# Four of the sixteen filter products of layer 2 on GpSimd, evictions moved from ScalarE to VectorE, and a new order of the items between the layers

## Chip, cores and metric

The kernel runs on one core of a Trainium2 chip. The metric is the device time of one execution in microseconds (us); the time of the kernel before is the median of three runs. The profile is of one further execution.

## What is computed

A sequence of 2048 rows of 448 bf16 values goes through two layers. Each layer has a spectral half (a two-dimensional Fourier transform of the normalized rows, a product with complex filter weights, the transform back, the residual) and a feed-forward half (448 to 1792, squared ReLU, back to 448, the residual). Both layers use the same weights.

```python
def _A_ref(x, w_r, w_i):
    X = rfft2(x)
    X = X * (w_r + 1j * w_i)
    return irfft2(X, s=(S, D))

def _B_ref(x, w1, b1, w2, b2):
    h = einsum("bsd,df->bsf", x, w1) + b1
    r = where(h > 0, h, 0)
    return einsum("bsf,fd->bsd", r * r, w2) + b2

x = x + _A_ref(layernorm(x), w_r, w_i)
x = x + _B_ref(layernorm(x), w1, b1, w2, b2)
x = x + _A_ref(layernorm(x), w_r, w_i)
x = x + _B_ref(layernorm(x), w1, b1, w2, b2)
```

## The kernel before

Everything stays in on-chip memory between the layers. The Fourier transforms are matmuls with constant matrices, split into stages, and each stage ends in PSUM and is copied ("evicted") to SBUF as bf16 by ScalarE (ACTIVATE, line 764) or VectorE (CAST, line 765). A layer runs through these stages:

- A: the transform of each tile of 128 rows along the sequence (`first_A` in layer 1, `second_A`, lines 1228 to 1245, in layer 2), 16 tiles, evicted into `XA`. In layer 2 tile 15 is evicted in two halves, and each half serves half of the columns.
- TD (`stage_TD`, line 934): the transform along the 448 columns, over 16 blocks n, alone or two at a time. It needs `XA` of all sixteen tiles. Evicted into `U`, a part of `arena`.
- B (`stage_B`, line 959): the rest of the sequence transform, two blocks at a time, evicted into `EF`, another part of `arena`.
- W (`stage_W`, line 988): the product with the filter, one instruction for each block n. It multiplies the 448 values of a block, read twice through a broadcast view, by 896 values of the weights `Wt`, both in SBUF, and writes 896 bf16 values into `T3`, a part of `wide`. In the kernel before all sixteen run on VectorE (line 793).
- Bi (`stage_Bi`, line 993): the first step back, for pairs of blocks v = 0 to 7. Bi v needs the two products n = 2v and 2v+1. Evicted into `VT`.
- TI, AI (lines 1019 and 1041): the rest of the way back; TI needs all of `VT`, that is, all eight Bi. Then the normalization (`ln_B`), the two feed-forward matmuls (`h_part`, `h_pairs`, `o_tile`) and the residual. The last tiles of this half (`o_tile`, then folding and statistics on VectorE) feed the next layer's A.

The text of the program only adds work units with their reads and writes; `_Sched` (line 297) puts them into queues. Each unit has a number, counted as the program adds it. The order on every engine is written out by hand in `ORDER` (line 140) as lists of these numbers, one list for each of TensorE ("pe"), ScalarE ("act"), VectorE ("dve"), GpSimd ("pool") and the DMA queue of SyncE ("sp"). An engine runs its list strictly in that order, and waits at a unit whose inputs are not there. A unit with an `alt` may stand in the list of any engine that its `alt` names; where the planner's own reckoning sees a gap on TensorE, it puts filler matmuls there (`warm_mm`, line 1375). The costs in the program are used for that reckoning, for the choice of PSUM banks and for the places of the waits; with the lists written out they do not choose the order.

The numbers of layer 2's spectral half, for following the prediction. Each TD, B and Bi unit is matmuls, and the number behind the slash is that of its eviction:

| stage | units (block: matmuls/eviction) |
|---|---|
| A, tile 15 | two halves: 815/816 and 817 |
| TD | 0: 818/819, 1: 820/821, 2-3: 822/823, 4-5: 833/834, 6-7: 835/836, 8-9: 845/846, 10-11: 847/848, 12-13: 857/858, 14-15: 859/860 |
| B | 0-1: 824/825, 826; 2-3: 829/830; 4-5: 837/838; 6-7: 841/842; 8-9: 849/850; 10-11: 853/854; 12-13: 861/862; 14-15: 865/866, 867 |
| W | n = 0 to 15: 827, 828, 831, 832, 839, 840, 843, 844, 851, 852, 855, 856, 863, 864, 868, 869 |
| Bi | v = 0: 870/871, 872; 1: 873/874; 2: 875/876; 3: 877/878; 4: 879/880; 5: 881/882; 6: 883/884, 885; 7: 886/887, 888 |

Evictions of two blocks have 896 elements a partition, of one block 448; those of a Bi have 1024, or 512 where it is evicted in two halves. In layer 2 before the change, the engines take these units in this order:

- ScalarE: 817 | 834, 860, 823, 850, 838, 836, 854, 825, 866, 858, 830, 880, 842, 882, 887, 862, 876, 872, 871, 878, 884
- VectorE: 816 | 846, 848, 821, 819, 852, 851, 867, 826, 869, 855, 868, 856, 839, 828, 840, 831, 827, 888, 843, 832, 844, 863, 864, 874, 885
- TensorE: 815 | 833, 845, 859, 847, 822, 849, 820, 818, 837, 853, 835, 865, 824, 879, 857, 829, 841, 881, 886, 875, 861, 870, 873, 877, 883

GpSimd's list holds nineteen units, all in layer 1: scalings of a constant matrix for `first_A` (line 776), memsets (line 806) and the four indirect DMAs that load the weights (line 842).

Of the kernel before, what the change touches and what calls it, by code (L numbers as in the profile page):

```python
# [6 lines left out]
ALU = mybir.AluOpType  # L7
# [11 lines left out]
LW = 224  # L19
# [14 lines left out]
def make_constants():  # L34
# [116 lines left out]
1261 1266 1233 1227 1271 1274 1277 1280 1283""",  # L151
    "act": """
# [11 lines left out]
1173 1165 1163 1170 1044 1237 1244 1242 1247 1239 1254 1252 1259 1269 1262 1249 1267 1264 1257""",  # L164
    "dve": """
# [22 lines left out]
1234 1278 1281 1284""",  # L188
    "pool": """
16 48 32 23 40 19 56 95 64 85 20 108 111 22 134 137 21 17 18""",  # L190
    "sp": """
8 9 10 11 12 13 14 15 24 25 26 201 202 141 142 143 144 146 222 223 224 145 225 226 227 272 276 277 294 312 330 348
366 384 934 939 940 957 975 1132 993 1135 1138 1011 1141 1029 1226 1232 1182 1047 1185 1188 1179 1229 1276 1273 1235
# [85 lines left out]
def _res(a):  # L279
    return a.ap() if isinstance(a, _PsAP) else a  # L280
# [350 lines left out]
def _free(ap):  # L631
    n = 1
    for step, cnt in list(ap.ap)[1:]:
        n *= cnt
    return n


def bass_interleave_layers__spectral_gfnet__dense_activation_squared_relu__prompt_kernel(nc, A_x, A_w_r, A_w_i, B_x, B_w1, B_b1, B_w2, B_b2, out):
# [5 lines left out]
    sch = _Sched()  # L644

    with ExitStack() as es:
# [16 lines left out]
        T3 = wide[:, 0:16 * TW].rearrange("p (n w) -> p n w", n=16)  # L663
# [127 lines left out]
        def tt(o, a, b, op, eng="dve"):  # L791
            rate = 0.96 if isinstance(a, _PsAP) or eng == "pool" else 1.92
            sch.add(eng, lambda e: e.tensor_tensor(o, _res(a), b, op), [a, b], [o], cost=_free(o) / rate + 69.0)  # L793
# [18 lines left out]
        def W_at(n):  # L812

            a = WS * 2 + (LW + 1) * (15 - n)
            o = Wt[:, (LW + 1) * n + 1:]
            return bass.AP(o.tensor, o.offset, [list(o.ap[0]), [a - (LW + 1) * n, 2], [WS, 2], [1, LW]])
# [117 lines left out]
        def stage_TD(n0, n, first):  # L934

            t = _Tile(n)
            u = sch.new_unit("pe")
            for i in range(n):
                for g in range(2):
                    for k in range(2):  # L940
                        x = XA[0:P if first else QD, k, g, 4 * (n0 + i):4 * (n0 + i) + 4].rearrange("p c t j -> p (c t j)")
                        if first:
                            r, m = 1 - g, TD_sb[:, g, k, :].rearrange("p (q i) -> p q i", q=2)
                            o = t[lambda b, i=i, r=r: ps[:, b + i, :].rearrange("p (q w) -> p q w", q=2)[:, :, r * QD:(r + 1) * QD]]
                        else:
                            r = (1 - k) if g == 0 else k
                            l0, m = g * 256 + r * QD, TQ_sb[:, g, r, :]
                            o = t[lambda b, i=i, l0=l0: ps[:, b + i, l0:l0 + QD]]
                        mm(o, x, m, g == 0 and k == 0, g == 1 and k == 1, skip=True, unit=u)
            TD_out(t, n0, n, EV["TD"])  # L950
# [34 lines left out]
                for i in range(2):  # L985
                    evac(EF[:, m0 + i, :], t[i][lambda b: ps[:, b, 0:2 * LW]], EV["B"])

        def stage_W(n):

            x = EF[:, n, :].rearrange("p (f l) -> p f l", f=2)[:, :, None, :].to_broadcast([P, 2, 2, LW])  # L990
            tt(T3[:, n, 0:4 * LW].rearrange("p (f w l) -> p f w l", f=2, w=2), x, W_at(n), ALU.mult)

        def stage_Bi(v):

# [257 lines left out]
        def spectral(first):  # L1252
            L = 0 if first else 1

            def rank(k, n):
                sch.bias, sch.tag = PR[k][L] - PR["step"][L] * n, f"{k}{L}.{n}"

            for g in range(4):
                n = 4 * g
                while n < 4 * g + 4:  # L1260
                    w = 2 if n in PAIRS else 1
                    rank("TD", n / 2)
                    stage_TD(n, w, first)
                    n += w
                for m0 in (4 * g, 4 * g + 2):
                    rank("B", m0 / 2)
                    stage_B(m0)
                    for m in (m0, m0 + 1):
                        rank("W", m / 2)
                        stage_W(m)  # L1270
            if first:
                sch.bias, sch.tag = 0.0, ""
                for i in range(2):
                    dma("sp", H_sb[:, 8 * i:8 * i + 8], dc["H"][:, 8 * i:8 * i + 8], after=[U[:, HGATE, 0:1]])
            for v in range(8):
                rank("Bi", v)
                stage_Bi(v)
# [190 lines left out]
```

## Time and profile before

| | |
|---|---|
| median of three runs | 253.97 us (253.86 to 254.29) |
| the profiled execution, its own time | 254.23 us |
| its span, first to last instruction | 252.4 us |
| layer 2, first TD matmul to last Bi matmul | 137.48 to 153.05 us of the span |
| first TI matmul of layer 2 | 153.94 us of the span |

All times inside the kernel are us from the start of the span. The profiled execution took 1.8 us longer than its span, and 0.26 us more than the median. A timeline row gives start, length, engine, source line, operation, output and input, and how many instructions it merges; neighbouring instructions of one engine overlap in the records a little, so the distance from start to start is shorter than the length of one. A group row ends in the busy time, the mean length of one in ns, the idle time before them and what ended it.

### The profile page before, as it was taken

What the parts mean: (1) busy time and instruction counts of PE and PEld (TensorE: products, weight loads), DVE (VectorE), ACT (ScalarE), POOL (GpSimd) and SP (SyncE); (2) the same over time, 40 slices, a digit from 0 to 9 for tenths busy, and PEclk for the clock granted to TensorE, in tenths of its full rate; (3) what the DMA queues carried; (4) which work ended last, traced back from release to release, by engine and by line L of the source; (5) the groups of instructions that cost most, each with busy time, mean ns of one, the idle gap of its engine ahead of it and who ended that gap; (6) DMA issues with size and microseconds to landing.
All of it is one profiled execution on the core that took longest, in us unless ns stands there. A gap on an engine that the chain in (4) does not pass through costs nothing.

```text
span 252.4 us, 6120 instructions
## 1 busy us (share of the span) xinstructions
PE 245.3 (97%) x2454; PEld 157.3 (62%) x2454; DVE 192.9 (76%) x624; ACT 164.2 (65%) x360; POOL 11.0 (4%) x23
## 2 busy tenths in 40 slices
PE   7999999999999999999998999999999999999996
PEld 2688688976446755544567688797544565544454
DVE  3988989999756789999997997999990398122632
ACT  6977979981468873209648998999638884017500
POOL 0880000000000000000000000000000000000000
PEclk9999999999999999999999999999999999999999
DMA  6988379515110001020000000031236010210002
GB/s 193 383 296 289 126 240 245 150 43 75 43 42 3 0 3 43 0 43 3 0 3 1 3 5 0 3 81 43 43 94 65 0 43 23 75 57 0 3 19 91
DMA packets 24080, 18.10 MB, mean 72 GB/s; under 512 B 16082, under 2 KB 22706, under 8 KB 24052
## 3 DMA queue, kind: packets, MB, share of 16 engines
q1 hardware_dynamic: 22756, 13.22, 20.7%
q0 software_dynamic: 576, 3.69, 4.0%
q10 hardware_dynamic: 720, 0.80, 1.0%
q8 instruction: 19, 0.31, 0.5%
q14 instruction: 9, 0.07, 0.1%
HBM read 12.20 MB, written 1.84 MB: 56 GB/s over the span
## 4 chain that ended last, share of the span: by engine, by line
PE 76%; DVE 12%; ACT 7%; DMA 3%; issue 1%
PE ps L739 76%; DVE wide L793 3%; DVE arena L765 3%; ACT XA L764 2%; DMA H_sb<-c_H 2%; DMA xin<-in_A_x_dram 1%; ACT arena L758 1%; ACT wide L764 1%; DVE x_sb L1224 1%; ACT Fs L775 1%; DVE st L864 1%; DVE VT L765 1%; ACT mv L758 1%; ACT wide L887 1%; ACT wide L886 1%
## 5 line engine op out<-in xcount | busy, mean ns | idle before, releaser
L739 PE MATMUL ps<-wide,W_sb 64*128 64x512 bf16 (+1 forms) x770 | 90.8, 346 | 0.0
L739 PE MATMUL ps<-W_sb,arena 128*128 128x448 bf16 (+3 forms) x476 | 87.0, 342 | 0.0
L758 ACT ACTIVATE arena<-ps,b1col 128x512 bf16<-128x512 f32 x84 | 52.8, 687 | 34.2 <-PE ps L739 33.9
L739 PEld LDWEIGHTS ps<-wide,W_sb 64*128 64x128 bf16 (+1 forms) x770 | 54.4, 95 | 32.5 <-ACT arena L758 0.7
L739 PEld LDWEIGHTS ps<-W_sb,arena 128*128 128x128 bf16 x476 | 45.5, 98 | 38.1 <-issue 0.8
L793 DVE TENSOR_TENSOR arena<-arena 128x512 bf16<-128x512 bf16 (+1 forms) x140 | 45.4, 367 | 18.2 <-ACT arena L758 18.1
L1102 ACT ACTIVATE VT<-x_sb 128x448 bf16<-128x448 bf16 x28 | 16.3, 587 | 10.8 <-DVE x_sb L1078 10.7
L764 ACT ACTIVATE arena<-ps 128x896 bf16<-128x896 f32 (+1 forms) x26 | 19.9, 852 | 4.1 <-PE ps L739 4.1
L758 ACT ACTIVATE mv<-mv,epst 128x1 f32<-128x1 f32 (+1 forms) x45 | 12.6, 293 | 12.8 <-DVE mv L865 12.6
L758 ACT ACTIVATE arena<-ps 128x256 bf16<-128x256 f32 x56 | 18.4, 399 | 2.9 <-PE ps L739 2.5
L1224 DVE SCALAR_TENSOR_TENSOR x_sb<-ps,mv,xin 128x448 bf16<-128x448 f32 (+2 forms) x13 | 8.2, 646 | 14.8 <-PE ps L739 14.7
L793 DVE TENSOR_TENSOR wide<-arena,Wt 128x896 bf16<-128x896 bf16 x32 | 17.7, 621 | 0.5 <-DMA Wt<-in_A_w_i_dram,ix 0.5
L739 PEld LDWEIGHTS ps<-H_sb,wide 64*128 64x128 bf16 x512 | 14.4, 94 | 3.4 <-DVE wide L793 1.0
L739 PE MATMUL ps<-H_sb,wide 64*128 64x128 bf16 x512 | 15.5, 216 | 0.8 <-DMA H_sb<-c_H 0.3
L739 PE MATMUL ps<-wide,VT 64*128 64x512 bf16 x42 | 15.8, 376 | 0.0
L764 ACT ACTIVATE wide<-ps 128x896 bf16<-128x896 f32 (+3 forms) x22 | 14.7, 724 | 1.6 <-PE ps L739 1.6
L764 ACT ACTIVATE XA<-ps 128x512 bf16<-128x512 f32 (+1 forms) x27 | 14.6, 594 | 0.5 <-PE ps L739 0.4
L764 ACT ACTIVATE VT<-ps 128x512 bf16<-128x512 f32 (+1 forms) x16 | 12.0, 825 | 0.6 <-PE ps L739 0.5
L1078 DVE SCALAR_TENSOR_TENSOR x_sb<-ps,mv,xin 128x448 bf16<-128x448 f32 x16 | 10.6, 680 | 1.9 <-PE ps L739 1.9
L765 DVE CAST arena<-ps 128x896 bf16<-128x896 f32 (+1 forms) x12 | 9.7, 852 | 2.3 <-PE ps L739 2.3
L1078 DVE SCALAR_TENSOR_TENSOR x_sb<-ps,mv,x_sb 128x448 bf16<-128x448 f32 x16 | 10.7, 681 | 0.6 <-PE ps L739 0.6
L739 PE MATMUL ps<-TI_sb,VT 112*128 112x112 bf16 (+1 forms) x128 | 10.0, 224 | 0.7 <-DVE VT L765 0.7
(76 smaller groups left out, 261.1 us busy)
## 6 DMA issues: line engine op xcount, KB each, us to landing
out_dram<-x_sb SPq DMA_DIRECT2D x15, 112.0 KB, 1.8
W_sb<-in_B_w_dram SPq DMA_DIRECT2D x1, 1568.0 KB, 12.8
H_sb<-c_H SPq DMA_DIRECT2D x2, 768.0 KB, 5.5
W_sb<-in_B_w_dram SPq DMA_DIRECT2D x1, 1344.0 KB, 6.1
xin<-in_A_x_dram SPq DMA_DIRECT2D x3, 224.0 KB, 5.1
G_sb<-c_G SPq DMA_DIRECT2D x1, 512.0 KB, 5.9
xin<-in_A_x_dram ACTq DMA_DIRECT2D x2, 224.0 KB, 4.8
VT<-in_B_w_dram SPq DMA_DIRECT2D x2, 192.0 KB, 3.2
```

Source lines behind the costliest of these rows:

```text
L739: return sch.add("pe", lambda e: e.matmul(_res(o), lhsT, rhs, start=start, stop=stop, skip_group_check=skip), [lhsT, rhs], [o], cost=cost, ...
L758: sch.add("act", lambda e: e.activation(o, _res(i), func, **kw), rd, [o], cost=c)
L764: op = sch.add(engs[0], lambda e: e.activation(o, _res(i), ACT.Copy) if h[0].eng == "act" else e.tensor_copy(o, _res(i)), [i], [o], cost=c ...
L765: e.tensor_copy(o, _res(i)), [i], [o], cost=c[engs[0]], unit=unit)
L775: op = sch.add(engs[0], lambda e: e.activation(o, i, ACT.Copy, scale=s) if h[0].eng == "act" else e.tensor_scalar(o, i, s, 1.0, op0=ALU.mu ...
L793: sch.add(eng, lambda e: e.tensor_tensor(o, _res(a), b, op), [a, b], [o], cost=_free(o) / rate + 69.0)
L864: small(lambda e, si=si, xi=xi: e.bn_stats(si, xi), [xi], [si], _free(xi) / 0.96 + 69.0)
L886: sch.add("act", lambda e: e.activation(o, xx, ACT.Copy, scale=1.0 / D, accum_out=m), [x], [o, m], cost=560.0)
L887: sch.add("act", lambda e: e.activation(o, xx, ACT.Square, bias=m, scale=-1.0, accum_out=v), [x, m], [o, v], cost=650.0)
L1078: small(lambda e, xx=xx, xi=xi, r=r, m=m: e.scalar_tensor_tensor(out=xx, in0=_res(r), scalar=m, in1=xi, op0=ALU.subtract, op1=ALU.add), [r ...
L1102: op = sch.add("act", lambda e, i=i, o=o, x=x, h=h: e.activation(o, x, ACT.Square, accum_out=sd[:, i, 1:2]) if h[0].eng == "act" else e.sc ...
L1224: small(lambda e: e.scalar_tensor_tensor(out=o, in0=_res(i), scalar=rs[0] if rs else 1.0, in1=xi, op0=ALU.add if t >= 4 and last else ALU. ...
```

## The change

`stage_W` gets its own call into the planner in place of the helper `tt`, with the same operation and operands, and in layer 2 an `alt` that allows GpSimd, booked at 2200 against VectorE's 536. The lists of `ORDER` are new from the last tiles of layer 1's feed-forward half to the first ones of layer 2's. Four products move to the "pool" list: those of blocks 8 (851), 12 (863), 5 (840) and 1 (828), in that order.

```diff
-        def stage_W(n):
+        def stage_W(n, first):

             x = EF[:, n, :].rearrange("p (f l) -> p f l", f=2)[:, :, None, :].to_broadcast([P, 2, 2, LW])
-            tt(T3[:, n, 0:4 * LW].rearrange("p (f w l) -> p f w l", f=2, w=2), x, W_at(n), ALU.mult)
+            o, w = T3[:, n, 0:4 * LW].rearrange("p (f w l) -> p f w l", f=2, w=2), W_at(n)
+            h = []
+            op = sch.add("dve", lambda e: e.tensor_tensor(o, x, w, ALU.mult), [x, w], [o], cost=536.0)
+            h.append(op)
+            if not first:
+                op.alt = {"dve": 536.0, "pool": 2200.0}
...
-                        stage_W(m)
+                        stage_W(m, first)
...
     "pool": """
-16 48 32 23 40 19 56 95 64 85 20 108 111 22 134 137 21 17 18""",
+16 48 32 23 40 19 56 95 64 85 20 108 111 22 134 137 21 17 18 851 863 840 828""",
```

In the lists, the part of layer 2's spectral half becomes (the units of other stages left out):

- ScalarE: 819, 858, 834, 848, 823, 862, 838, 830, 880, 854, 878, 826, 866, 825, 885, 884, 867, 876, 882, 872, 888
- VectorE: 817, 816 | 846, 836, 850, 860, 842, 852, 843, 844, 839, 864, 821, 832, 856, 831, 855, 868, 827, 874, 869, 871, 887
- TensorE: 815 | 845, 818, 857, 835, 833, 849, 847, 822, 859, 861, 841, 837, 853, 829, 879, 820, 877, 883, 824, 865, 875, 873, 881, 870, 886
- GpSimd: 851, 863, 840, 828

Against the order before, VectorE takes from ScalarE the evictions 817 (256 elements), 836, 842, 850, 860 (896 each), 871 and 887 (512 each), and gives it 848 (896), 819, 826, 867 (448 each), 885 and 888 (512 each). Outside this half VectorE also takes three small copies from ScalarE (903, 916 and 990, in `ln_B`). Ahead of it, some of the evictions of stage A change places on ScalarE; behind it, the items of TI, AI, `ln_B` and the first quarter of the feed-forward half (units 890 to 1141) stand in a new order on TensorE, ScalarE and VectorE. The DMA queues' lists are the same.

More of the change, by code (lines that the diff above doesn't have):

```diff
@@ L158 @@
 381 471 581 720 511 718 596 725 676 611 728 706 723 661 735 691 730 740 738 733 745 743 748 750 481 756 576 771 496
[5 rows of a table removed]
-1173 1165 1163 1170 1044 1237 1244 1242 1247 1239 1254 1252 1259 1269 1262 1249 1267 1264 1257""",
[5 rows of a table added]
+1044 1237 1244 1242 1247 1239 1254 1252 1259 1269 1262 1249 1267 1264 1257""",
     "dve": """
```

32 rows, old and new, of the table ORDER are left out of this document.

## The prediction

> **What bounds the kernel now.** I read the page's busy shares first, then the chain that ended last, then the timelines of VectorE, ScalarE and TensorE in the stretch that the change touches.
>
> ```profile
> PE 245.3 (97%) x2454; PEld 157.3 (62%) x2454; DVE 192.9 (76%) x624; ACT 164.2 (65%) x360; POOL 11.0 (4%) x23
> ```
> ```profile
> 137.34 0.14 issue
> 137.48 0.96 PE ps L739 x16
> 138.46 2.32 DVE arena L765 x3
> ...
> 141.68 1.07 DVE wide L793 x2
> 142.75 1.07 DVE arena L765 x2
> 143.81 4.84 DVE wide L793 x9
> 148.65 0.61 DVE VT L765
> ...
> 149.30 3.78 PE ps L739 x128
> ...
> 153.94 0.95 PE ps L739 x12
> ...
> 157.86 92.20 PE ps L739 x701
> ```
> ```profile
> 137.40:153.90 16.50, 15.57 (x388) 12.13 (x388) 15.30 (x25) 15.80 (x22) 0.00 (x0) 1.00 0.01 3
> 157.90:250.00 92.10, 92.10 (x701) 53.58 (x701) 56.43 (x167) 51.77 (x121) 0.00 (x0) 1.00 0.19 42
> ```
>
> TensorE is the bound of the whole (97%), but not of layer 2's spectral half: there the chain of waits runs through VectorE from 138.46 to 149.26, eleven of its steps products, and only then through four Bi on TensorE. The columns of the stretches are length, then busy time of PE, weight loads, DVE, ACT and POOL, the granted clock and DMA: in 16.5 us VectorE works 15.30 and ScalarE 15.80, GpSimd nothing. Behind it, from 157.9 on, TensorE is busy 92.10 of 92.10 us. So a shift of the spectral half's end (TI starts at 153.94) is passed on nearly whole to the end of the kernel.
>
> **The change: what it moves between VectorE and ScalarE.** The timelines, and the groups by shape:
>
> ```profile
> 143.73 4.92 DVE L793 TENSOR_TENSOR wide<-arena,Wt 128x896 bf16<-128x896 bf16 x9
> ```
> ```profile
> 138.07 5.78 ACT L764 ACTIVATE arena<-ps 128x896 bf16<-128x896 f32 x7 [0.49 <-PE ps L739]
> ```
> ```profile
> L793 DVE TENSOR_TENSOR wide<-arena,Wt 128x896 bf16<-128x896 bf16 x32 | 17.7, 621 | 0.5 <-DMA Wt<-in_A_w_i_dram,ix 0.5
> L764 ACT ACTIVATE arena<-ps 128x896 bf16<-128x896 f32 x20 | 17.4, 935 | 4.1 <-PE ps L739 4.1
> L764 ACT ACTIVATE VT<-ps 128x512 bf16<-128x512 f32 x9 | 5.1, 632 | 0.5 <-PE ps L739 0.5
> L765 DVE CAST arena<-ps 128x896 bf16<-128x896 f32 x6 | 6.3, 1087 | 2.3 <-PE ps L739 2.3
> L765 DVE CAST VT<-ps 128x1024 bf16<-128x1024 f32 x3 | 3.7, 1219 | 0.0
> L765 DVE CAST arena<-ps 128x448 bf16<-128x448 f32 x6 | 3.5, 617 | 0.0
> L764 ACT ACTIVATE arena<-ps 128x448 bf16<-128x448 f32 x6 | 3.3, 577 | 0.0
> L765 DVE CAST VT<-ps 128x512 bf16<-128x512 f32 x3 | 2.1, 689 | 0.1
> L765 DVE CAST XA<-ps 128x256 bf16<-128x256 f32 x3 | 1.2, 422 | 0.5 <-PE ps L739 0.5
> L764 ACT ACTIVATE XA<-ps 128x256 bf16<-128x256 f32 x1 | 0.4, 398 | 0.0
> ```
>
> Neighbours overlap, so I cost by the distance from start to start: a product (4.92 - 0.62) / 8 = 0.54 us, that is its length less 0.08; an ACTIVATE of 896 (5.78 - 0.93) / 6 = 0.81, its length less 0.12. With the same overlaps a CAST is 1.01 for 896 elements, 1.14 for 1024, 0.61 for 512, 0.54 for 448, 0.34 for 256; an ACTIVATE 0.51 for 512, 0.46 for 448, 0.28 for 256.
>
> VectorE loses four products, 2.16. It takes 817, four of 896 and two of 512 (0.34 + 4.04 + 1.22 = 5.60) and gives 848, three of 448 and two of 512 (1.01 + 1.62 + 1.22 = 3.85). Net -0.41 us. ScalarE gives 0.28 + 3.24 + 1.02 = 4.54 and takes 0.81 + 1.38 + 1.02 = 3.21: -1.33 us. The three small copies of ln_B lie under the full TensorE stretch at 157.9 and later; I cost them at nothing, and without that cover they would be some 0.3 us each on VectorE. The same cover holds the new order of TI, AI and the first feed-forward quarter; if it leaked, each wait there would show as TensorE idle time behind 157.9, which is none now.
>
> **Where those microseconds lie.** TensorE's timeline has the places where it waits, and its rates:
>
> ```profile
> 144.18 0.57 PE L739 MATMUL ps<-TQ_sb,XA 112*128 112x112 bf16 x8
> 144.68 0.95 PE L739 MATMUL ps<-arena,G_sb 64*64 64x448 bf16 x16
> 145.76 2.85 PE L739 MATMUL ps<-H_sb,wide 64*128 64x128 bf16 x96
> ```
>
> Three Bi take 2.85 with 0.16 of overlap: 0.90 each; two B 0.95: 0.40 each; a TD 0.39, and about 0.1 lies at each change from one kind to another (11 changes before, 8 in the new list: -0.3). A hand-over from one engine to TensorE takes 0.14 (the first row of the chain above).
>
> Walk through the new lists with GpSimd beside VectorE undisturbed and 2.1 us a product (below). TD starts at 137.45 as now. Its first tile goes to VectorE, so 846 starts at 138.05 instead of 138.46; 846, 836, 850, 860, 842 at 1.01 each end at 143.1. 850 lands at 141.15 and GpSimd runs 851 until 143.3, behind casts. The first Bi (879) needs 851 and 852: 852 ends at 143.7, so it starts at 143.85, later than now (143.2 before). VectorE then does five products, 821 and four products until 148.5, 868 and 827 until 149.7 (their inputs 866 and 825 come off ScalarE at about 148.5 and 148.9). GpSimd: 863 until 145.4, 840 until 147.5, 828 (its input 826 lands at 148.05) from 148.2 to 150.3. TensorE: 879, 820, 877, 883, 824, 865, 875, 873, 881 without a gap until 150.6, 870 at once. The last Bi (886) needs product 869, which VectorE's list puts behind the eviction 874 of Bi 1: 873 ends 149.9, 874 151.0, 869 151.6, so 886 runs 151.75 to 152.8, its halves are out at 153.55, TI starts at 153.7. That is 0.25 earlier than now; with the first Bi as early as before (143.2) it would be 0.9.
>
> **What a product costs on GpSimd.** No row shows one with two inputs. The rows nearest to it:
>
> ```profile
> L776 POOL TENSOR_SCALAR Fs<-FA_sb,rstd 128x256 bf16<-128x256 bf16 x11 | 5.1, 476 | 6.0 <-DVE m L878 5.8
> L806 POOL MEMSET W_sb<- 128x896 f32 x1 | 0.9, 860 | 0.0
> L806 POOL MEMSET wide<- 128x256 f32 x1 | 0.3, 319 | 0.0
> ```
>
> Lower end: the one-input scaling of 256 elements, 476 ns, with 640 more at the memsets' (860 - 319) / 640 = 0.85 ns: 1.0 us. Upper end: 476 scaled to 896, twice for two inputs: 3.3 us. I take 2.1, twice the lower end, two inputs read in turn. [...]
>
> **What a product on GpSimd does to VectorE.** This decides the case, and the trace does not show it. GpSimd's reads of SBUF all lie in layer 1's start, beside instructions of VectorE with one input:
>
> ```profile
> 10.00 0.92 POOL L776 TENSOR_SCALAR Fs<-FA_sb,rstd 128x256 bf16<-128x256 bf16 x2
> ```
> ```profile
> 10.44 0.59 DVE L864 BATCH_NORM_STATS2 st<-xin 128x6 f32<-128x448 bf16 x1
> ...
> 11.17 0.59 DVE L864 BATCH_NORM_STATS2 st<-xin 128x6 f32<-128x448 bf16 x1
> ```
>
> The one at 10.44 has a scaling beside it for most of its length and takes 0.59, like the one at 11.17 that has it beside less: with one input nothing is lost. VectorE's products have two inputs in SBUF, and from 143.1 on they are its whole work, back to back. The bounds: no loss (the walk above), or full exclusion, where of two products on the two engines one stands still until the other ends. A gain is excluded, since nothing of a product gets shorter by company.
>
> Full exclusion at 2.1 us, a waiting product going next: 852 waits until 143.3; 863 runs 143.9 to 146.0; 843; 840 146.6 to 148.7; 844; then 839, 864, 821 until 150.9, which is 4.6 later than in the free walk, and B 0-1 (824), queued on TensorE with all Bi but three behind it, waits for 821. 826 follows at 152.5, 828 runs 152.6 to 154.7, in front of 855, 868, 827 (156.3), 874 (157.4), 869 (158.0), Bi 7 (159.1), its eviction (159.8), TI at 159.95: 6.0 later than now. If VectorE instead keeps going while it has products, 863 starts only beside the cast 821, 840 in the next gap, and Bi 6 and Bi 2 wait for them on TensorE: TI at 158.5, 4.5 later. At 1.0 us a product the first walk gives 156.2, 2.3 later. Between 2.3 and 6.0, and by the middle walk, I take +4.0.
>
> [...]
>
> **Forecast.** The exclusion: 253.97 + 4.0 = 258.0 us. (The profiled execution would then be at 258.2, by its 0.26 above the median; its span 256.4.) Chance 0.50: nothing in the rows speaks against it, VectorE's eleven products behind 143.1 stand in its list with one cast between them, and it needs no special value of the GpSimd product.
>
> **Rivals.** Side by side at full rate: -0.25 by the walk, up to -0.8 if the first Bi is not late; with the fewer changes of kind I put it at 253.5. For it: one-input rows show no loss, and ScalarE and VectorE are the full engines of this stretch. Against: the first Bi comes later in the new list, and GpSimd's fourth product ends 0.2 us before TensorE needs it. Chance 0.40, of which a little more than half (0.22) is over 0.2%, 0.17 within, 0.01 beyond.
>
> GpSimd merely slow: no exclusion, but 3.3 us a product. Then 851 ends at 144.5, 863 147.8, 840 151.1, 828 154.4: Bi 2 waits until 151.2 and Bi 0 until 154.5, TI at 157.1, so 257.1. It decides from about 2.3 us a product (four in a row behind 141.2 then end past 150.6); 2.8 gives +1.1. For it: the row of 476 ns scaled twice; against: the memsets' flat rate. Chance 0.10, 0.09 of it slower.
>
> **The numbers.** Slower: 0.50 x 0.95 + 0.09 + 0.01 = about 0.57. Faster: 0.22, and 0.01 from an exclusion that is mild and falls beside casts: 0.23. Same: 0.20. A difference under 0.2% (0.5 us) can't be told from none. The range reaches from 253.2 (the free walk at -0.8) to 260.0 (the exclusion at +6.0); I leave about 0.06 below and 0.12 above, where a TensorE pause of some 4 us (145 to 149 in the first exclusion walk) might also lower the granted clock, which is 1.00 in both stretches now. The forecast's own range is 256.3 to 260.0.
>
> **What would show it.** Right: gaps of one to two us between VectorE's products exactly where a GpSimd product runs (or products stretched to over 1 us, if the record counts the wait), TensorE waiting for `wide` in front of Bi, TI's start near 158. The free walk is right if all twelve products keep 621 ns and 0.54 from start to start beside GpSimd, with TI at 153.1 to 153.7. The slow rival shows as GpSimd products of about 3 us, VectorE unstretched, TensorE waiting for POOL. Idle time on TensorE behind the start of the full stretch would prove me wrong on the cover of the rest. The forecast falls if TI starts before 155.

## The result, and the profile after

The changed kernel takes 258.94 us (median of six, 257.55 to 260.06) against 253.95 beside it on the same chip: a ratio on record of 1.0173, 95% interval 1.0149 to 1.0197 (the two medians alone give 1.0196). It is slower, by the mechanism that was forecast, and 0.9 us beyond the forecast 258.0.

The profiled execution took 259.19 us with a span of 257.4. The first TD starts where it did (137.38, before 137.48); TI starts at 158.21 instead of 153.94. From here on "the stage" is the stretch from the first TD matmul to the first TI matmul, and "the end" what is left of the span behind it. The stage went from 16.46 to 20.83 us, the end from 98.5 to 99.2.

The page's first part for the kernel after; against before, GpSimd has 7.3 us more and VectorE 5.1 us more, though it runs four products fewer:

```profile
PE 247.9 (96%) x2455; PEld 156.6 (61%) x2455; DVE 198.0 (77%) x624; ACT 161.8 (63%) x356; POOL 18.3 (7%) x27
```

Where VectorE's time comes from stands in the groups: the row of its products (now line 993) had 32 of 621 ns, has 28 of 768, and there are four new ones on GpSimd. The same view cut to the stage shows the twelve of layer 2 alone, 962 ns each:

```profile
L993 DVE TENSOR_TENSOR wide<-arena,Wt 128x896 bf16<-128x896 bf16 x28 | 19.9, 768 | 1.1 <-ACT arena L764 1.1
L993 POOL TENSOR_TENSOR wide<-arena,Wt 128x896 bf16<-128x896 bf16 x4 | 7.3, 1845 | 128.3 <-PE ps L739 122.9
```
```profile
L993 DVE TENSOR_TENSOR wide<-arena,Wt 128x896 bf16<-128x896 bf16 x12 | 10.9, 962 | 1.1 <-ACT arena L764 1.1
```

The mean hides the shape: nine of the twelve keep 0.61 to 0.62 us, and three are three times as long. The timelines of GpSimd and of VectorE, in narrow windows so that rows do not merge:

```profile
141.14 1.81 POOL L993 TENSOR_TENSOR wide<-arena,Wt 128x896 bf16<-128x896 bf16 x1 [122.86 <-PE ps L739]
142.98 1.69 POOL L993 TENSOR_TENSOR wide<-arena,Wt 128x896 bf16<-128x896 bf16 x1
142.98 3.74 POOL L993 TENSOR_TENSOR wide<-arena,Wt 128x896 bf16<-128x896 bf16 x2
152.18 1.79 POOL L993 TENSOR_TENSOR wide<-arena,Wt 128x896 bf16<-128x896 bf16 x1 [5.45 <-ACT arena L764]
```
```profile
142.17 1.08 DVE L765 CAST arena<-ps 128x896 bf16<-128x896 f32 x1
143.16 1.99 DVE L993 TENSOR_TENSOR wide<-arena,Wt 128x896 bf16<-128x896 bf16 x1
143.16 4.04 DVE L993 TENSOR_TENSOR wide<-arena,Wt 128x896 bf16<-128x896 bf16 x2
152.56 1.88 DVE L993 TENSOR_TENSOR wide<-arena,Wt 128x896 bf16<-128x896 bf16 x1 [1.06 <-ACT arena L764]
```

Read the two together. 851 (141.14) runs beside casts, and casts are not held: 1.08 us at 142.17. Then GpSimd's 863 starts at 142.98 and ends at 144.67; VectorE's 852 starts at 143.16 and ends at 145.15 (143.16 + 1.99), 0.48 us behind it. 840 was issued at 144.63 (its record is 2.09 us long, against some 1.75 undisturbed) and is held in turn until 852 is out: it ends at 146.72 (142.98 + 3.74). VectorE's 843 ends at 147.20 (143.16 + 4.04), 0.48 behind that. The record counts the wait into the length of the instruction. The fourth, 828, ends at 153.97, and 868 at 154.44, 0.47 behind. In all these rows a product runs on one engine or on the other, never on both.

TensorE's timeline shows what that did, and the stretches the granted clock (last columns but two):

```profile
143.46 0.62 PE L739 MATMUL ps<-H_sb,wide 64*128 64x128 bf16 x16
145.21 0.62 PE L739 MATMUL ps<-H_sb,wide 64*128 64x128 bf16 x16 [1.13 <-DVE wide L993]
145.77 0.32 PE L739 MATMUL ps<-TQ_sb,XA 112*128 112x112 bf16 x3
147.26 0.22 PE L739 MATMUL ps<-TQ_sb,XA 112*128 112x112 bf16 x1 [1.18 <-DVE wide L993]
147.42 3.24 PE L739 MATMUL ps<-H_sb,wide 64*128 64x128 bf16 x64
...
155.04 2.29 PE L739 MATMUL ps<-H_sb,wide 64*128 64x128 bf16 x65 [0.41 <-DVE wide L993]
158.21 1.71 PE L739 MATMUL ps<-TI_sb,VT 112*128 112x224 bf16 x24 [0.29 <-DVE VT L765]
164.07 0.23 PE L739 MATMUL ps<-J_sb,x_sb 128*128 128x128 bf16 x1 [0.20 <-DVE x_sb L793]
```
```profile
137.38:147.86 10.48, 8.09 (x160) 5.62 (x162) 9.97 (x10) 8.15 (x10) 5.55 (x3) 1.00 0.01 2
147.86:151.27 3.41, 3.41 (x64) 2.90 (x62) 3.41 (x7) 1.02 (x1) 0.00 (x0) 0.50 0.02 5
151.27:158.21 6.94, 6.23 (x177) 4.98 (x170) 5.61 (x7) 5.86 (x10) 1.79 (x1) 1.00 0.01 2
```

Three waits for products, 2.72 us together. Behind the second, the clock is 0.50 for 3.41 us, so that two Bi (147.42, 64 matmuls) take 3.24 instead of the 1.96 that two take elsewhere at full clock (at 155.67 in e4, at 27.64 in the kernel before). And the row at 164.07 is TensorE idle behind the start of the full stretch: a leak where the prediction had allowed none.

### The profile page after: what moved, and what is told of

Same layout as the page of the kernel before. It is cut to its first block, busy times and chain, and to the rows that moved or that the text cites. A ratio compares the mean times of both kernels' runs of the same rounds, so it can differ in the third digit from the quotient of the medians.

```text
span 257.4 us, 6124 instructions
## 1 busy us (share of the span) xinstructions
PE 247.9 (96%) x2455; PEld 156.6 (61%) x2455; DVE 198.0 (77%) x624; ACT 161.8 (63%) x356; POOL 18.3 (7%) x27
## 4 chain that ended last, share of the span: by engine, by line
PE 79%; DVE 11%; ACT 7%; DMA 1%; issue 1%
PE ps L739 79%; DVE wide L993 2%; ACT XA L764 2%; DMA xin<-in_A_x_dram 1%; DVE wide L793 1%; ACT arena L758 1%; DVE x_sb L1229 1%; DVE st L864 1%; ACT Fs L775 1%; DVE arena L765 1%; ACT wide L887 1%; ACT mv L758 1%; DVE Fs L776 1%; ACT wide L886 1%; DVE arena L793 1%
## 5 line engine op out<-in xcount | busy, mean ns | idle before, releaser
L739 PEld LDWEIGHTS ps<-wide,W_sb 64*128 64x128 bf16 (+1 forms) x770 | 52.5, 95 | 33.9 <-ACT arena L758 1.4
L764 ACT ACTIVATE arena<-ps 128x896 bf16<-128x896 f32 (+1 forms) x26 | 18.8, 803 | 6.0 <-PE ps L739 6.0
L993 DVE TENSOR_TENSOR wide<-arena,Wt 128x896 bf16<-128x896 bf16 x28 | 19.9, 768 | 1.1 <-ACT arena L764 1.1
L739 PE MATMUL ps<-H_sb,wide 64*128 64x128 bf16 x512 | 17.5, 226 | 1.6 <-DVE wide L993 1.5
L739 PEld LDWEIGHTS ps<-H_sb,wide 64*128 64x128 bf16 x512 | 15.6, 99 | 4.1 <-DVE wide L993 2.2
L993 POOL TENSOR_TENSOR wide<-arena,Wt 128x896 bf16<-128x896 bf16 x4 | 7.3, 1845 | 128.3 <-PE ps L739 122.9
L764 ACT ACTIVATE wide<-ps 128x896 bf16<-128x896 f32 (+3 forms) x20 | 14.0, 753 | 1.4 <-PE ps L739 1.4
L764 ACT ACTIVATE XA<-ps 128x512 bf16<-128x512 f32 x26 | 14.4, 603 | 0.5 <-PE ps L739 0.5
L765 DVE CAST arena<-ps 128x896 bf16<-128x896 f32 (+1 forms) x12 | 11.1, 967 | 1.6 <-PE ps L739 1.5
L1152 DVE RECIPROCAL rstd<-mv 128x2 f32<-128x2 f32 x12 | 1.9, 161 | 11.7 <-ACT mv L758 11.6
```

The lines of the kernel that those rows point to most:

```text
L739: return sch.add("pe", lambda e: e.matmul(_res(o), lhsT, rhs, start=start, stop=stop, skip_group_check=skip), [lhsT, rhs], [o], cost=cost, ...
L764: op = sch.add(engs[0], lambda e: e.activation(o, _res(i), ACT.Copy) if h[0].eng == "act" else e.tensor_copy(o, _res(i)), [i], [o], cost=c ...
L765: e.tensor_copy(o, _res(i)), [i], [o], cost=c[engs[0]], unit=unit)
L993: op = sch.add("dve", lambda e: e.tensor_tensor(o, x, w, ALU.mult), [x, w], [o], cost=536.0)
```

## The experiments

Theory: two-input products on VectorE and GpSimd exclude each other, and that is the loss. Rivals: GpSimd is slow or late in itself; the new order of the lists is the loss. Twelve kernels were run, each beside the kernel before (253.8 to 254.1 us). The start of the stage differs between executions, up to 2.8 us in the table below, mostly because one of layer 1's first three Bi waits for the DMA of the constants `c_H` for a time that varies: not at all in seven of the fourteen traces, 1.19 us in e9, 2.57 in e2. What is left of the differences, up to 0.7 us (e7 starts 0.94 later than the kernel after and waits 0.25), is not accounted for. TensorE's rows of e2, then of e9:

```profile
28.53 1.07 PE L740 MATMUL ps<-H_sb,wide 64*128 64x128 bf16 x32 [2.57 <-DMA H_sb<-c_H]
```
```profile
29.79 1.07 PE L738 MATMUL ps<-H_sb,wide 64*128 64x128 bf16 x32 [1.19 <-DMA H_sb<-c_H]
```

That moves everything behind it, and lies over 100 us ahead of the change. So the lengths of stage and end, which it does not touch, are compared beside the times:

| kernel | TD | TI | stage | end | time, us (median) | ratio |
|---|---|---|---|---|---|---|
| before | 137.48 | 153.94 | 16.46 | 98.5 | 253.95 | |
| after | 137.38 | 158.21 | 20.83 | 99.2 | 258.94 | 1.0173 (1.0149 to 1.0197) |
| e1, all products on VectorE | 137.19 | 155.00 | 17.81 | 99.2 | 256.01 | 1.0084 (1.0067 to 1.0101) |
| e2, GpSimd only writes | 139.93 | 155.61 | 15.68 | 99.2 | 254.19 | 1.0007 (0.9996 to 1.0018) |
| e3, VectorE with one input | 137.34 | 153.02 | 15.68 | 99.2 | 254.04 | 1.0022 (1.0005 to 1.0039) |
| e4, old lists, four on GpSimd | 137.36 | 159.81 | 22.45 | 98.3 | 260.12 | 1.0255 (1.0229 to 1.0282) |
| e5, only 851 on GpSimd | 137.38 | 155.23 | 17.85 | 99.2 | 256.30 | 1.0098 (1.0077 to 1.0119) |
| e6, fillers in the pauses | 138.34 | 157.81 | 19.47 | 99.2 | 258.53 | 1.0167 (1.0147 to 1.0188) |
| e7, old lists behind | 138.32 | 159.14 | 20.82 | 98.3 | 258.03 | 1.0142 (1.0112 to 1.0173) |
| e8, 851 and 828 on GpSimd | 138.68 | 156.81 | 18.13 | 99.2 | 256.81 | 1.0102 (1.0085 to 1.0119) |
| e9, as e5, booked short, old lists behind | 138.78 | 156.76 | 17.98 | 98.3 | 256.59 | 1.0082 (1.0050 to 1.0114) |
| e10, as e1, booked short | 137.15 | 155.67 | 18.52 | 99.2 | 257.09 | 1.0129 (1.0094 to 1.0165) |
| e11, as e5, fillers left out | 137.40 | 155.29 | 17.89 | 99.2 | 256.60 | 1.0103 (1.0073 to 1.0133) |
| e12, as e11, old lists behind | 137.84 | 155.74 | 17.90 | 98.3 | 256.56 | 1.0110 (1.0077 to 1.0144) |

**Is it the two inputs? (e2, e3.)** e2 keeps every list and leaves out GpSimd's four products; two memsets stand in each one's place, so GpSimd still writes but reads nothing from SBUF, and the results of these four blocks are zero. e3 keeps GpSimd's products and takes the second input from VectorE: its twelve products of layer 2 become statistics of the same block of `EF`, and their results are left out. (The code is shortened.)

```diff
+ if h[0].eng == "pool":                       # e2
+     e.memset(z, 0.0)
+     return e.memset(o, 0.0)
+ return e.bn_stats(st[:, n, 0:6], EF[:, n, :])  # e3, VectorE in layer 2
```

> The changed kernel with each GpSimd product replaced by two memsets that read nothing from SBUF (1.3 to 1.7 us together, about what a product took less its waits); the four blocks' results are zeros. Exclusion of SBUF reads: VectorE's products keep 0.62 us beside them, no pause of TensorE over 0.5 us, TI at 153.5 to 154.2, 253.5 to 254.8 us (the 0.6 us lost behind the stretch stays). Rival, GpSimd merely slow or late in the order of the Bi: hardly any change, 256.5 us or more. Rival, any GpSimd activity stops VectorE: products stretched to over 1 us, 256.5 or more.

> The changed kernel with VectorE's twelve products of layer 2 replaced by BN_STATS of the same block (one input in SBUF, about 0.6 us, as long as a product); GpSimd's four products stay as they are. Those twelve blocks' results are left out. Exclusion needs two inputs on VectorE: nothing stretched, GpSimd products 1.65 to 1.85 us each, TI at 153.5 to 154.2, 253.5 to 254.8 us. Rival, GpSimd merely slow: as the changed kernel, 256.5 or more, since GpSimd does the same work in the same order. Rival, any read on VectorE collides: BN_STATS stretched to 1.5 to 2.1 us, 256.5 or more.

In e2 VectorE's products are back at 619 ns; in e3 GpSimd does the same four products as in the kernel after, and VectorE's twelve one-input instructions take 611 ns beside them. The groups, of e2 and of e3:

```profile
L1000 DVE TENSOR_TENSOR wide<-arena,Wt 128x896 bf16<-128x896 bf16 x12 | 6.7, 619 | 0.0
```
```profile
L996 DVE BATCH_NORM_STATS2 st<-arena 128x6 f32<-128x448 bf16 x12 | 6.6, 611 | 0.0
L995 POOL TENSOR_TENSOR wide<-arena,Wt 128x896 bf16<-128x896 bf16 x4 | 7.0, 1753 | 124.4 <-PE ps L739 122.8 <-ACT arena L764 1.6
```

Take away either side's part in it, GpSimd's reads or VectorE's second input, and the stage is 15.68 us, 5.15 less than after and 0.78 less than before. That shows the exclusion and prices it (the lowered clock, which neither run has, is in the price). Both times lie in the ranges given (253.5 to 254.8 us); the start of TI does not: it is 0.5 earlier than given in e3, and in e2 it comes late with a stage that began 2.55 later.

e3 takes more than the second input away: its statistics also write 6 values instead of 896. That the wide write is not what collides is shown by two other rows: in e2 both engines write 896 values side by side and VectorE keeps 619 ns, and in the kernel after VectorE's cast at 142.17 writes 896 values into SBUF beside GpSimd's 851 and takes its usual 1.08 us. What these runs do not separate is the second input as such from the larger amount that is read with it.

The slow rival falls with e3: GpSimd's work is all there, at 1.75 us each, and nothing waits for it. So VectorE's products lost time beside GpSimd's products (1.88 to 2.13 us for the three held ones of the kernel after) and none beside its writes alone (619 ns), and VectorE's one-input instructions lost none beside GpSimd's products (611 ns). What in the chip causes it, no run shows.

**The lists or the engine? (e1, e4.)** e1 keeps the new lists and puts the four products back on VectorE, 851 behind 852, 840 behind 839, 863 behind 864, 828 behind 827. e4 keeps the lists of before and takes the same four products out of VectorE's.

```diff
- 16 48 32 ... 17 18 851 863 840 828    # pool list of e1
+ 16 48 32 ... 17 18
- 16 48 32 ... 17 18                    # pool list of e4, other lists as before
+ 16 48 32 ... 17 18 851 828 840 863
```

> The new lists with the four products back on VectorE (851 behind 852, 840 behind 839, 863 behind 864, 828 behind 827), nothing on GpSimd in layer 2. Exclusion theory: no product of VectorE is longer than 0.62 us, and what is left is VectorE's own 2.16 us more of work in the stretch: 254.3 to 255.5 us, TI of layer 2 starting at 154.3 to 155.3. Rival, the new lists themselves cost the time: 258 to 259 us, TI near 158. Rival, GpSimd merely slow: as the exclusion theory.

> The lists of before on TensorE, ScalarE and VectorE, only the four products taken out of VectorE's list and put on GpSimd (851, 828, 840, 863). Exclusion theory: here 851 is ready just when VectorE begins its products, so all four collide; each costs VectorE 1.2 to 1.5 us and saves it 0.54: 256.5 to 259.5 us. Rival, the new lists are to blame: VectorE is relieved of 2.16 us, 253 to 254.2 us. Rival, GpSimd merely slow: 254 to 256, no product of VectorE over 0.7 us.

In e4 three of the four collisions came as expected; in the fourth GpSimd's product was the held one, and VectorE's lost nothing. The time is 0.6 above the range. The range had no lowered clock in it, and e4 had one in all four executions (0.987 to 0.993), which alone is more than the 0.6 (some 1.4 us, by e6 below). Its stage is 1.62 longer than that of the kernel after, whose profiled execution had the lowered clock as well. GpSimd's and VectorE's timelines of e4:

```profile
141.38 1.80 POOL L992 TENSOR_TENSOR wide<-arena,Wt 128x896 bf16<-128x896 bf16 x1 [123.05 <-ACT arena L763]
144.81 4.16 POOL L992 TENSOR_TENSOR wide<-arena,Wt 128x896 bf16<-128x896 bf16 x2 [1.63 <-DVE arena L764]
155.62 2.13 POOL L992 TENSOR_TENSOR wide<-arena,Wt 128x896 bf16<-128x896 bf16 x1 [6.66 <-ACT arena L763]
```
```profile
141.47 2.19 DVE L992 TENSOR_TENSOR wide<-arena,Wt 128x896 bf16<-128x896 bf16 x1
144.65 6.94 DVE L992 TENSOR_TENSOR wide<-arena,Wt 128x896 bf16<-128x896 bf16 x7
155.58 0.63 DVE L992 TENSOR_TENSOR wide<-arena,Wt 128x896 bf16<-128x896 bf16 x1 [0.51 <-ACT arena L763]
```

There even 851 meets a product (141.47, 2.19 us), which the new lists avoid by putting casts beside it, and seven products take 6.94 instead of the 3.84 of seven undisturbed ones in e5. e1 missed its range by 0.5 on the high side. No product is stretched there (sixteen of 619 ns), but the new order asks for eight products before its third Bi (883 needs 863), and VectorE now makes all eight in a row: 883 starts 10.23 us into the stage. The new lists without GpSimd lose 1.35 in the stage and 0.7 behind it. So the new order costs time in the stage when VectorE has to make all sixteen products; with four of them off VectorE and no collision it gains 0.78 there (e2, e3). Behind the stage it loses 0.7 in either case.

**How much does one collision cost? (e5, e8.)** e5 gives GpSimd 851 alone, which runs beside casts; e8 adds 828, which meets products.

```diff
- 851 863 840 828    # end of the pool list
+ 851                # e5; 863, 840, 828 behind 864, 839, 827 on VectorE
+ 851 828            # e8
```

> The new lists, 851 alone on GpSimd (it ran beside the casts 860 and 842), the other three products back on VectorE (840 behind 839, 863 behind 864, 828 behind 827). Exclusion theory: 851 meets no product of VectorE, so it costs nothing and saves 0.54 us against the new lists without GpSimd (256.01): 255.2 to 255.8 us, no product over 0.7 us. Rival, every product on GpSimd costs its over 1 us wherever it lies: 256.5 or more.

> The new lists, 851 and 828 on GpSimd, 863 and 840 back on VectorE. Exclusion theory: 828 starts while VectorE is among its last products; one of them is stretched to 1.8 to 2.2 us, so against the kernel with 851 alone plus 1.3 less 0.54: 256.0 to 257.0 us. Rival, the loss of the changed kernel is not additive but a jam of the first two collisions: 255.2 or less.

In e8 828 took 2.00 us and stretched 868. VectorE's timeline:

```profile
150.37 0.62 DVE L993 TENSOR_TENSOR wide<-arena,Wt 128x896 bf16<-128x896 bf16 x1
151.02 2.09 DVE L993 TENSOR_TENSOR wide<-arena,Wt 128x896 bf16<-128x896 bf16 x1
```

That is 1.48 us lost on VectorE against 0.54 saved, and of the net 0.94 only 0.28 reached the stage (18.13 against 17.85). e8 is as expected. e5 is not: 851 costs VectorE nothing and GpSimd 1.80 us, yet the stage is no shorter than e1's and the time 0.5 above the range.

**Was it the fillers? (e9 to e12.)** In e5 the planner puts nine filler matmuls between Bi 4 and Bi 2, four of them straight ahead of Bi 2, whose products are ready. My first explanation was that they eat the spared product. e9 and e10 book the products so short that the planner sees no gap; e11 and e12 leave bookings and waits as in e5 and only leave out the nine matmuls.

```diff
- op.alt = {"dve": 536.0, "pool": 2200.0}
+ op.alt = {"dve": 100.0, "pool": 700.0}    # e9 (e5 with e7's lists), e10 (e1)
...
+ if op in drop:                            # e11 (e5), e12 (with e7's lists)
+     continue
```

> Only product 851 on GpSimd, the products booked so short that the planner sets no filler matmuls into the stage, and behind the last Bi the lists of before. If the nine fillers ate the product that VectorE was spared (0.36 us of wait of eviction 874, up to 0.54), the stage (first TD to first TI) is 17.3 to 17.5 us and the rest 98.3: about 254.4 to 254.8 us. If the new lists bound the stage by something else, it stays at 17.85 and the time is 255.0 to 255.3. By neither is it faster than the kernel before.

> All sixteen products on VectorE, the new lists throughout, no filler matmuls in the stage. If VectorE's chain sets the stage here, it stays at 17.8 us and the time at about 256.0 (255.7 to 256.2). If the fillers had delayed it as in the run with one product, the stage is 17.3 to 17.5 and the time 255.3 to 255.6.

> As the run with product 851 alone on GpSimd, with the same bookings and the same places of the waits, but the nine filler matmuls between Bi 4 and Bi 2 left out. In that run five fillers ended at 147.02 and Bi 6 waited for product 863 anyway, so these five cost nothing; the four at 148.95 to 149.72 stood in front of Bi 2, whose inputs were there. If they ate the spared product, the stage is 17.0 to 17.5 us instead of 17.85 and the time 255.4 to 256.0. If VectorE's chain through the eviction 874 and product 869 sets the end, the stage stays within 0.1 of 17.85 and the time at 256.2 to 256.5.

> The same, with the lists of before behind the last Bi: the best version that the runs so far point to. The end is 98.30 us behind TI instead of 99.17, so 0.87 less than the run beside it: 254.5 to 255.1 if the fillers ate the spared product, 255.3 to 255.7 if not. Not faster than the kernel before either way, whose stage is 16.46.

The explanation falls, and all four are above their ranges (e11 by 0.1, the others by 0.9 to 1.3). e9 and e10 could not test it: with other bookings the program also moves a wait for VectorE's cast 821 forward onto Bi 6, and TensorE waits 0.31 for it there (the stages got longer, by 0.13 and 0.71; the 0.31 is not all of e10's). e11 does test it, and its stage is 17.89. Where the fillers stood, TensorE now waits, and the wait has a name:

```profile
147.08 1.07 PE L739 MATMUL ps<-H_sb,wide 64*128 64x128 bf16 x32 [1.23 <-DVE wide L993]
148.08 0.96 PE L739 MATMUL ps<-arena,G_sb 64*64 64x448 bf16 x18
149.85 4.64 PE L739 MATMUL ps<-H_sb,wide 64*128 64x128 bf16 x160 [0.82 <-ACT arena L764]
```

Bi 2 (149.85) waits not for products but for ScalarE's evictions of the two B just ahead of it (826 and 866, the second starting at 149.17 and 0.54 long). In e5's plan Bi 2 gets the PSUM banks that these two hold; in the kernel after it gets those of Bi 3, long evicted. Five Bi then run without a gap to the end of the stage. So Bi 2 is held by a PSUM bank that the planner, with other engines and bookings, gave out differently; the fillers only covered the wait. That this is where the spared product went is argued and was not run: VectorE's eviction 874 (its row in e11 is below) waits 0.41 us for TensorE, so an earlier Bi 2 could give back at most that much of the 0.54 before VectorE's own chain sets the end again.

```profile
151.85 1.22 DVE L765 CAST VT<-ps 128x1024 bf16<-128x1024 f32 x1 [0.41 <-PE ps L739]
```

e12, the best version that the runs pointed to, is not faster than before: its stage of 17.90 against 16.46 outweighs 98.3 against 98.5. Its end is 0.9 shorter than e11's, but its median is no more than 0.04 lower: in its profiled execution the stage starts 0.44 later, and the other three have spans of 254.5 to 255.8 without a profile.

**The lowered clock (e6).** The planner is told how long the stretched products are, so that it puts fillers (42 instead of 25 in the kernel) into TensorE's pauses.

```diff
- op.alt = {"dve": 536.0, "pool": 2200.0}
+ op.alt = {"dve": {10 - 1: 1990.0, 6: 2130.0, 14: 2350.0}.get(n, 536.0), "pool": 1750.0}
```

> The changed kernel, with the planner told what the trace shows: 1990, 2130 and 2350 for the products 852, 843 and 868 on VectorE, 1750 for one on GpSimd. The four lists stay; it only puts filler matmuls into TensorE's pauses (six ahead of Bi 4, five ahead of Bi 3, four ahead of Bi 0). Theory, the pauses lower the granted clock and that costs 1.4 us where it happens: granted clock 1.000 in every execution, 257.3 to 257.9 us. Rival, the lowered clock hides behind VectorE's waits: 258.5 or more with clock 1.000. Rival, fillers delay the Bi: over 259.

The granted clock was 1.00 in all its executions, and the stage 19.47, 1.36 less. The profiled execution began the stage 0.96 later (0.7 of waiting for `c_H`), and the median is 0.6 above the range; the clock went as expected, the time did not. The fillers also changed the last collision (828 was held there, not 868), so the 1.36 need not be the clock's alone. Its size agrees with the executions of the kernel after: those at a mean clock of 1.000 took 257.55 and 257.65, those at 0.993 took 258.94 to 259.19 (half the clock for 3.41 us of 257.4 is 0.993), one at 0.987 took 260.06.

**The order behind the stage (e7).** The kernel after up to the last Bi, with the lists of before behind it and the three copies of `ln_B` back on ScalarE.

> The changed kernel up to the last Bi, with the items behind it (units from 890 on) in the order of the kernel before. Theory, the new order behind the spectral half loses 0.7 us by itself: from TI's start to the end of the span 98.4 to 98.6 us instead of 99.2, 258.0 to 258.5 us. Rival, that loss comes from the late half: no change, 258.7 to 259.3.

The end is 98.3 instead of 99.2, as expected, with a stage of 20.82. The median of 258.03 us lies just inside its range, and the clock had a part in that: two of e7's four executions ran at a mean clock of 0.999 or 1.000 (256.98 and 257.52 us), of the kernel after only two of six (257.55 and 257.65); at 0.993 e7 took 258.54 and 259.25, about what the kernel after takes there (258.94 to 259.19). The same lists behind the stage stand in e9 and e12: their ends are 0.9 shorter than those of e5 and e11, but their medians are not (256.59 against 256.30, 256.56 against 256.60); their profiled executions begin the stage 1.40 and 0.44 later. So the 0.9 is shown by the pieces of the traces (98.3 in four traces with the old lists behind, 99.2 in all nine with the new ones), and not by the times. Which of the order and the copies makes it was not tried apart. The kernel after shows two of the places, which are not the whole of it: the 0.20 us at 164.07, where VectorE is late with `x_sb`, and a filler where the kernel before has none:

```profile
196.19 1.02 PE L739 MATMUL ps<-wide,W_sb 64*128 64x512 bf16 x6
197.14 0.39 PE L1381 MATMUL ps<-ones 128*128 128x512 bf16 x1
197.46 1.03 PE L739 MATMUL ps<-wide,W_sb 64*128 64x512 bf16 x7
```

## Why the prediction was right, and where it was not

**The account.** Against the span of before (+5.0): the exclusion 5.15 (20.83 - 15.68, the lowered clock in it), the gain that the change would have had without it -0.78, the order behind the stage +0.7, and a stage that began 0.1 earlier.

**The mechanism** held: products stretched to some 2 us exactly where a GpSimd product runs, TensorE waiting for `wide` in front of Bi, TI near 158. What the trace of before could not show, a second input on VectorE beside GpSimd, is what e2 and e3 took away. That one of two products stands still until the other has ended was a bound of the prediction, not shown by a row of before; the rows after show it, with ends 0.47 to 0.48 us apart.

**The shift of +4.0** against 4.27 measured is closer than its parts. The fully worked walks assumed 2.1 us a product; undisturbed ones took 1.69 to 1.81. They let the whole queue of products slip behind 828; in the trace 828 met only 868. On the other side the lowered clock was named as a possibility, behind a pause of some 4 us (the longest in the stage of any trace is 1.67, in e4), and left out of the sum; it is about 1.4 of the 4.27 (1.36 by e6, 1.3 to 1.6 between the executions at 1.000 and 0.993). Without it TI moves by 2.9: within the 2.3 to 6.0 that were given, but well below the middle. Two errors of opposite sign met, so the nearness of +4.0 is luck.

**Who goes first** was left open between two orders of service. Both occur. In the kernel after the engines take turns. In e6 828 took 3.53 us, while six products of VectorE in a row took 3.30, no more than six beside writes alone (3.31 in e2); then a cast, beside which GpSimd could run, and the next product was the held one. GpSimd's timeline and VectorE's:

```profile
151.67 3.53 POOL L993 TENSOR_TENSOR wide<-arena,Wt 128x896 bf16<-128x896 bf16 x1 [3.98 <-ACT arena L764]
```
```profile
150.25 3.30 DVE L993 TENSOR_TENSOR wide<-arena,Wt 128x896 bf16<-128x896 bf16 x6
153.47 1.21 DVE L765 CAST VT<-ps 128x1024 bf16<-128x1024 f32 x1
154.61 1.08 DVE L993 TENSOR_TENSOR wide<-arena,Wt 128x896 bf16<-128x896 bf16 x1
```

**The free walk's -0.25, up to -0.8**, was mis-sized as a forecast of that case: the stage gained 0.78, the outer end, and not by the condition named for it. The first Bi was not as early as before; it began 6.09 us into the stage of e3 against 5.70. The gain came behind it, with products of 1.75 us where the walk had 2.1. The same trace also shows why this version would not be faster without collisions: e3 gives the gain back behind the stage (98.5 to 99.2) and measures 254.04.

**"I cost them at nothing"** is the step that failed: the new order behind the stage, and the three copies, cost 0.7 us against the kernel before and 0.9 against e7, by the ends in the traces. A TensorE at 92.10 of 92.10 us busy was read as a cover for any order of the items under it. It covers other engines' work only while TensorE has something ready, and the order, which decides that, was changed too. The 0.7 is most of the 0.9 by which the forecast fell short; where all of it lies was not traced. The sign in the profile that the prediction named for it, idle time behind the start of the full stretch, is the row at 164.07; the filler at 197.14 shows that such a leak can also look busy.

## What to carry to other kernels

Before moving a two-input SBUF operation to GpSimd, look at what VectorE does at that time: beside casts from PSUM (1.08 us at 142.17) or one-input instructions (611 ns in e3) it cost VectorE nothing here; beside VectorE's own two-input products it was not parallel work but the same work at a third of the speed (1.75 us against 0.62), in VectorE's way. When comparing versions, split the span at a matmul that all have, and compare the pieces; a transfer that varies ahead of it would otherwise hide or feign a microsecond. When the planner fills gaps, a busy TensorE may be a waiting one: leave the fillers out to see what it waits for.

## What was not expected of the hardware

The exclusion goes by whole instructions in these traces and is not a slowing of both: a held VectorE product ends 0.47 to 0.49 us behind GpSimd's, and an instruction may be held for as long as it runs (828 in e6: 3.53 us, of which some 1.75 are its own). VectorE's products kept their turn there while they stood back to back (starts 0.54 apart); in e8, where one started a little late (0.65 behind the one ahead of it, 150.37 and 151.02), GpSimd got in between. A small gap is not what decides, though: in e4 VectorE's second product stood back to back with the one that started at 144.65, so its turn was at 145.19 (an estimate, by the 0.54 from start to start in e5), and GpSimd's, issued at 144.81, got in between all the same: TensorE waited 1.55 us for the second, until 147.45. What decides who goes next stays open.

The clock halved without a long pause: two waits of 1.13 and 1.18 us, their ends 2.05 apart, and 0.50 for 3.41 us behind them; by their mean clocks this happened in four of the six executions. No pause in the kernel after was longer than 1.18 us. In e4 and e7, at a mean clock of 0.993 as well, the waits ahead of the stretched Bi are 1.55 and 1.67 us, and 1.13 and 1.17. The length of a pause alone does not decide: e2's TensorE waits 2.57 us in one piece (for `c_H`, until 28.53), and its mean clock is 1.000.

The trace of the kernel after shows more of the condition. The clock is full for 143.36 us from 4.50 on, then half for 3.41, then full for 105.81, then 0.51 in the 0.32 us that are left of the span; the two full stretches are 42 and 31 times 3.413. Divided into slices of that length, the 252.58 us from 4.50 to 257.08 have two in which TensorE is busy for less than half: 1.47 us (144.45 to 147.86) and 1.36 us (253.67 to 257.08, where TensorE's work ends). Behind both the clock is half. The other 72 have 2.49 us or more, and behind them it is full. What lies between 1.47 and 2.49 this trace leaves open. If the slices lie otherwise against the waits in another execution, the same waits can fall into one slice or be split between two, which would explain four executions of six. This is a reading of one trace; no run moved the waits against the slices by itself.
